# RWKV attention, Fourier mix and MLP on one core: ScalarE copies transposes as fp32 words, batch 3's transform in half columns, a new order

## Chip, core and metric

The kernel runs on one core of one Trainium2 chip. The metric is the device time of one execution in microseconds (us), the median of three runs. The engines are TensorE (PE; its weight loads are shown as PEld), VectorE (DVE), ScalarE (ACT), GpSimd (POOL) and SyncE (SP), which here only issues DMAs.

## The reference

Four batches, 8 heads, 768 positions, head size 48 (model size 384). A linear attention with decay gives x; then a Fourier mix over positions and model dimension, a layer norm and a two-layer MLP:

```python
cur = np.einsum('bhd,bhe->bhde', u[None] * kt, vt)
y[:, :, t] = np.einsum('bhd,bhde->bhe', rt, state + cur)
state = wt[:, :, :, None] * state + np.einsum('bhd,bhe->bhde', kt, vt)
...
X = np.fft.fft(x, axis=1)
X = np.fft.fft(X, axis=2)
u = x + np.real(X).astype(np.float32)
mu = np.mean(u, axis=-1, keepdims=True)
var = np.mean((u - mu) ** 2, axis=-1, keepdims=True)
un = (u - mu) / np.sqrt(var + 1e-06)
ch = np.maximum(un @ w_ch1, 0.0) @ w_ch2
return (u + ch).astype(np.float32)
```

## The kernel before

A program of some 1400 operations is written as data and then put out engine by engine. `op(engine, duration, function, r=..., w=...)` adds one; `r` and `w` name what it reads and writes, and from them the waits on semaphores follow. An operation may have alternatives on several engines. `ORDER` at the top lists for each engine (pe, act, dve, pool, sp) the numbers of its operations in the order in which they are put out; so it also says which engine does what. The durations in the text serve only to choose PSUM banks and the order of waits; the chip sees the order. Every engine works its list strictly in order.

**Start.** `small_constants`, `tables`, `sines`, `masks`, `fills`, `mirrors` and `tables_end` make the cosine and sine tables CS and SS, the identity IDW and its negative NIDW, masks and zero padding; ScalarE loads one activation table for the sines (L1079) and a second for Ln and Exp (L683). PE first runs 16 matmuls on a filled part of W1 (L1086) and later, between other work, `NW` warm matmuls (L1118) whose results nobody reads.

**Attention** (`attention`, 24 chunks of 128 positions, six to a batch): loads of w, k, r, v by SP (L597); Ln of w on ScalarE; two matmuls that sum it (L761, L765) and two Exp; rk = r k u with its sum dc (POOL or DVE); rh = r times the one Exp (L799), kh = k times the other. rh and kh are transposed: for the first 18 chunks by PE (L815, L821), with a bf16 copy from PSUM to `rkt` by `evict` (L574 on ScalarE, L575 on VectorE); for the last six by a DMA (L807). Then scores (L831), their mask (L836, ah), the state (L857, L865), the output y (L887) and x (L896, called addX here, or a copy). `fold` adds and subtracts halves of x into xf.

**Mix** (`mix`, one batch): three tables' transform over positions on PE (L953 to L956), evicted to hcs and mirrored to hcr; then for each of six blocks kb of 128 positions the model-dimension transform: three matmuls of 384 columns (L980, j = 0, 1, 2) on the tables DTM. VectorE adds x with a sum over the row (L985, uf), un is uf less its mean (ScalarE or VectorE), ScalarE also squares it. un is transposed, in batches 0 and 1 by PE (L1015) and `evict`, in 2 and 3 by one DMA for three blocks (L1021) to `unt`. Then the up matmuls (L1044) for three blocks at once, ht = relu (L1052 on ScalarE, L1050 on VectorE), the down matmuls (L1063, four at a time), osb (L1069) and the out DMA (L1073). Attention of the next batches is mixed in between by the order.

Of the kernel before, what the change touches and what calls it, by code (L numbers as in the profile page):

```python
# [7 lines left out]
ALU = mybir.AluOpType  # L8
# [24 lines left out]
NW = 32  # L33

YPE = (0, 1, 2, 3, 4)

# [5 lines left out]
        "7 68 1414 1415 1416 60 95 97 94 122 1417 124 1418 62 106 121 107 149 1419 64 110 151 113 1420 134 "  # L42
        "133 1421 1422 148 176 115 137 178 1423 1424 1425 1426 116 160 175 142 140 161 203 188 205 187 1427 "
        "143 164 1428 191 1429 263 167 1430 169 202 230 1431 170 215 1432 1433 229 196 197 214 194 1434 241 "
        "1435 1436 218 240 421 423 221 420 223 244 1437 224 479 1438 1439 255 1440 256 257 247 264 450 449 "
        "258 265 432 452 481 259 271 272 1441 273 274 275 276 277 266 278 260 279 267 280 461 281 282 268 "
        "301 433 285 293 294 295 302 1442 286 287 303 1443 311 491 327 312 299 328 313 319 320 462 291 321 "
        "1444 307 436 465 329 343 339 341 317 347 1445 337 325 345 333 359 478 355 353 382 392 386 507 394 "
        "351 398 439 378 508 510 519 380 349 357 490 442 376 384 520 542 494 390 388 396 366 541 468 367 471 "
        "544 368 523 371 553 574 497 575 372 554 361 362 529 526 557 405 500 585 406 586 363 764 373 560 562 "  # L50
        "589 765 767 407 410 794 796 793 411 400 592 776 401 615 599 402 805 783 777 412 600 601 616 780 617 "
        "602 618 603 619 604 620 621 622 607 608 822 609 610 611 623 624 625 626 612 823 637 825 629 655 630 "
        "638 852 639 645 854 631 646 656 647 812 806 835 657 834 643 671 663 672 673 635 664 651 665 838 809 "
        "886 888 689 683 687 691 703 685 864 681 669 695 885 786 851 693 699 841 701 815 697 897 863 705 661 "
        "898 919 706 867 901 707 715 844 677 870 918 873 1098 716 1099 1101 730 717 930 728 724 904 726 1125 "
        "722 929 906 734 710 1114 933 1177 711 1179 1127 1124 1151 1153 951 712 952 738 936 1111 720 740 959 "
        "742 960 953 1208 732 736 1210 943 961 1140 962 1150 963 944 1137 964 965 966 945 967 968 946 954 "
        "955 947 948 969 970 956 744 745 1166 1176 746 985 979 986 987 980 973 974 981 749 1006 975 1000 "
        "1238 1001 1007 1008 1002 994 995 996 750 754 1117 751 1189 1163 755 756 1023 1019 1237 1031 1025 "
        "1029 1021 1143 1015 1074 1068 1207 1195 1192 1033 1060 1056 1017 1169 1058 1062 1064 1037 1066 1249 "  # L60
        "1220 1072 1223 1027 1076 1035 1039 1259 1225 1040 1044 1045 1252 1049 1054 1050 1041 1260 1070 1261 "
        "1267 1262 1268 1263 1264 1275 1078 1276 1277 1269 1278 1279 1280 1281 1282 1283 1270 1284 1285 1286 "
        "1271 1272 1083 1289 1290 1316 1301 1291 1302 1295 1303 1296 1297 1079 1317 1318 1322 1323 1088 1051 "
        "1089 1310 1324 1311 1090 1084 1046 1080 1331 1347 1312 1335 1343 1337 1333 1085 1345 1339 1351 1341 "
        "1349 1370 1353 1386 1355 1365 1360 1366 1361 1372 1356 1376 1390 1384 1378 1374 1357 1380 1382 1367 "
        "1394 1362 1392 1388 1395 1399 1404 1400 1396 1401 1405 1406 1409 1410 1411"),
    "act": (
# [1084 lines left out]
```

## Time and profile before

| | before |
|---|---|
| median of three runs | 184.25 us (183.04, 184.25, 184.69) |
| profiled execution: time | 183.65 us |
| profiled execution: span from first to last instruction | 181.8 us |
| busy: PE, DVE, ACT, POOL | 175.5, 150.2, 130.1, 107.8 us |
| granted TensorE clock | 1.00 throughout |
| HBM read and written | 23.59 and 4.72 MB |

The difference between the profiled execution's time and its span lies before the first and after the last instruction. A form's row gives line, engine, operation, what it writes and reads, count, busy us and mean ns of one. Matmul ends are modelled in the profile, and a matmul's own duration contains time in which the next one already runs; how fast they follow each other is read from their starts.

### The profile page before, as it was taken

To read this page: it belongs to the slowest core of one execution; us is meant where nothing else is said; L and a number is where in the kernel's file an instruction comes from. 1 tells how busy PE (TensorE), PEld (TensorE's weight loads), DVE (VectorE), ACT (ScalarE), POOL (GpSimd) and SP (SyncE) were. 2 spreads that over 40 slices of the span, in tenths; PEclk is the share of its full clock that TensorE was granted. 3 is DMA by queue.
4 is the path that set the end of the run, shared out by engine and by line. 5 is a ranking of instruction groups with operands and counts; after the bars stand their busy time and mean duration, and the time that the engine had idled before them with its cause. 6 is when DMAs were issued, how large, how long until landed. Compare 5 with 4: busy or idle time off the path is not lost.

```text
span 181.8 us, 4574 instructions
## 1 busy us (share of the span) xinstructions
PE 175.5 (97%) x1718; PEld 115.8 (64%) x1718; DVE 150.2 (83%) x351; ACT 130.1 (72%) x323; POOL 107.8 (59%) x127
## 2 busy tenths in 40 slices
PE   4999999999999999999999999999999999999994
PEld 2466766766666776776767666665656766666663
DVE  8989999988988999999899998999799941860434
ACT  2879899499987876899999985977972455481410
POOL 3059888798324999587989987799763220000000
PEclk9999999999999999999999999999999999999999
DMA  6999999999997989898999999999640004360033
GB/s 126 218 217 214 184 215 194 180 211 187 170 206 140 221 174 260 185 221 192 224 224 189 221 164 222 170 232 188 88 85 0 5 0 108 107 176 1 0 130 130
DMA packets 116119, 28.99 MB, mean 159 GB/s; under 512 B 111361, under 2 KB 116098, under 8 KB 116098
## 3 DMA queue, kind: packets, MB, share of 16 engines
q1 hardware_dynamic: 114514, 26.36, 71.4%
q0 software_dynamic: 1584, 2.36, 7.7%
q8 instruction: 13, 0.21, 0.5%
q14 instruction: 8, 0.07, 0.1%
HBM read 23.59 MB, written 4.72 MB: 156 GB/s over the span
## 4 chain that ended last, share of the span: by engine, by line
PE 72%; DMA 7%; POOL 6%; DVE 5%; ACT 4%; SPq 3%; issue 3%; DVEq 0%; POOLq 0%; ACTq 0%
PE bank L1063 23%; PE bank L1044 19%; PE bank L980 5%; DMA rkt<-rkh 5%; PE bank L1086 3%; PE bank L831 3%; PE bank L956 2%; PE bank L1118 2%; POOL rk L551 2%; POOL rkh L551 2%; DMA in_r<-in_r_dram 2%; SPq L597 2%; PE bank L815 2%; PE bank L887 2%; PE bank L877 1%
## 5 line engine op out<-in xcount | busy, mean ns | idle before, releaser
L1063 PE MATMUL bank<-w,ht 128*128 128x384 bf16 (+2 forms) x300 | 54.0, 319 | 0.0
L1044 PE MATMUL bank<-unt,w 128*128 128x384 bf16 x288 | 53.6, 326 | 0.0
L1052 ACT ACTIVATE ht<-bank 128x384 bf16<-128x384 f32 x71 | 32.9, 500 | 16.3 <-PE bank L1044 15.9
L1063 PEld LDWEIGHTS bank<-w,ht 128*128 128x128 bf16 x300 | 27.7, 98 | 15.6 <-ACT ht L1052 0.2
L1044 PEld LDWEIGHTS bank<-unt,w 128*128 128x128 bf16 x288 | 26.7, 98 | 15.9 <-DVE osb L1069 0.4
L836 DVE TENSOR_TENSOR ah<-bank,msk 128x512 bf16<-128x512 f32 x48 | 31.1, 682 | 0.8 <-PE bank L831 0.5
L551 POOL TENSOR_TENSOR rkh<-in_k,e 128x384 bf16<-128x384 f32 x20 | 20.2, 1012 | 15.1 <-ACT e L780 12.4
L551 POOL TENSOR_TENSOR rk<-rk,ub 128x384 f32<-128x384 f32 x21 | 21.5, 1027 | 5.4 <-DVE rk L551 5.0
L1069 DVE SCALAR_TENSOR_TENSOR osb<-bank,rstd,uf 128x384 f32<-128x384 f32 (+2 forms) x25 | 14.8, 597 | 10.3 <-PE bank L1063 9.0
L551 POOL TENSOR_TENSOR vtd<-in_v,dc 128x384 f32<-128x384 f32 x21 | 17.6, 842 | 4.9 <-DMA in_v<-in_v_dram 3.0
L551 POOL TENSOR_TENSOR rk<-in_r,in_k 128x384 f32<-128x384 f32 x18 | 18.7, 1047 | 2.1 <-DMA in_r<-in_r_dram 2.1
L1050 DVE TENSOR_SCALAR ht<-bank 128x384 bf16<-128x384 f32 x25 | 13.3, 550 | 7.9 <-PE bank L1044 7.8
L985 DVE SCALAR_TENSOR_TENSOR uf<-bank,x 128x384 f32<-128x384 f32 x24 | 12.9, 553 | 2.9 <-PE bank L980 2.4
L565 ACT ACTIVATE xf<-uf,agg 128x384 bf16<-128x384 f32 x24 | 14.7, 616 | 0.6 <-DVE uf L985 0.6
L551 POOL TENSOR_TENSOR sd<-x 128x385 f32<-128x385 f32 x12 | 12.8, 1089 | 3.3 <-DVE x L896 3.2
L799 DVE TENSOR_TENSOR rkh<-bank,in_r 128x384 bf16<-128x384 f32 x24 | 13.2, 548 | 1.0 <-ACT bank L767 1.0
L780 ACT ACTIVATE e<-bank 128x392 f32<-128x392 f32 (+1 forms) x24 | 11.9, 498 | 2.7 <-PE bank L774 1.2
L767 ACT ACTIVATE bank<-bank 128x384 f32<-128x384 f32 x24 | 11.8, 496 | 2.6 <-PE bank L761 2.4
L788 DVE TENSOR_REDUCE dc<-rk 128x8 f32<-128x384 f32 x24 | 12.8, 543 | 1.1 <-POOL rk L551 1.1
L574 ACT ACTIVATE rkt<-bank 128x512 bf16<-128x512 bf16 x21 | 12.5, 602 | 1.6 <-PE bank L821 1.6
L565 ACT ACTIVATE lb<-in_w 128x384 bf16<-128x384 f32 x24 | 12.5, 529 | 1.3 <-DMA in_w<-in_w_dram 1.2
L565 ACT ACTIVATE un<-uf,agg 128x384 bf16<-128x384 f32 x18 | 10.2, 607 | 2.3 <-DVE uf L985 2.3
(138 smaller groups left out, 352.4 us busy)
## 6 DMA issues: line engine op xcount, KB each, us to landing
in_w<-in_w_dram SPq DMA_DIRECT2D x24, 192.0 KB, 3.8
in_k<-in_k_dram SPq DMA_DIRECT2D x24, 192.0 KB, 3.8
in_r<-in_r_dram SPq DMA_DIRECT2D x24, 192.0 KB, 3.8
in_v<-in_v_dram SPq DMA_DIRECT2D x24, 192.0 KB, 4.0
out_dram<-osb SPq DMA_DIRECT2D x23, 192.0 KB, 2.6
w<-in_moe_w_ch_dram POOLq DMA_DIRECT2D x2, 576.0 KB, 7.9
w<-in_moe_w_ch_dram POOLq DMA_DIRECT2D x1, 1152.0 KB, 12.0
out_dram<-osb SPq DMA_DIRECT2D x1, 128.0 KB, 1.7
```

The costliest lines, as they stand in the source:

```text
L551: return lambda e: e.tensor_tensor(out=o, in0=a, in1=b, op=f)
L565: return lambda e: e.activation(o, a, f, **kw)
L574: {"act": lambda e: e.activation(o(), i(), ACTF.Copy), "dve": lambda e: e.tensor_copy(out=o(), in_=i())}, **kw)
L788: op("dve", v_1(DM), lambda e: e.tensor_reduce(out=dc[:, :], in_=rku[:, :, :], axis=mybir.AxisListType.X, op=ALU.add), r=[("RK", i2)], w=[ ...
L799: op("dve", v_1(DM), lambda e: e.tensor_tensor(out=rh[:, :, 0:D], in0=ps(tce)[:, 0:DM].rearrange("t (h d) -> t h d", d=D), in1=rt[:, :, :] ...
L836: masked[n] = op("dve", v_1(512), lambda e, x=x: e.tensor_tensor(out=ah[:, x:H:2, :], in0=ps(ta[x])[:, :].rearrange("p (h t) -> p h t", t= ...
L985: op("dve", v_1(DM) + 60, lambda e, kb=kb, t=t: e.scalar_tensor_tensor(out=uf[:, kb, :], in0=ps(t)[:, 0:DM], scalar=1.0, in1=xb[:, kb, 0:D ...
L1044: ins = e.matmul(ps(t)[:, 0:384], W1[:, m, 256 * (j // 2) + j % 2:256 * (j // 2) + 256:2], unt[:, :, m, :], start=(m == 0), stop=(m == NM ...
L1050: {"dve": lambda e, j=j, t=t, ht=ht: e.tensor_scalar(out=ht[:, j, :], in0=ps(t)[:, 0:384], scalar1=su, scalar2=0.0, op0=ALU.mult, op1=ALU. ...
L1052: "act": lambda e, j=j, t=t, ht=ht: e.activation(ht[:, j, :], ps(t)[:, 0:384], ACTF.Relu, scale=su)},
L1063: ins = e.matmul(ps(t)[:, 0:hi - lo], ht[:, j, 128 * x:128 * x + 128], W2[:, j, lo:hi], start=(j == 0), stop=(j == NJ - 1))
L1069: op("dve", v_1(hi - lo) + 64, lambda e, kb=kb, t=t, o=o, lo=lo, hi=hi: e.scalar_tensor_tensor(out=o[:, lo:hi], in0=ps(t)[:, 0:hi - lo], s ...
```

## The change

1. `evict` on ScalarE: where the copy is bf16 to bf16 (x = 2), input and output are taken as fp32, so two bf16 values travel as one word and the instruction has half as many elements. The identity IDW is now also made by such a copy, on ScalarE, from NIDW, which VectorE fills with the identity first.
2. Table steps (TQ, zero fills, the mirrored tables, the negated ones and NIDW) get a ScalarE alternative. The two activation-table loads get a fence: each waits for the instruction before it on ScalarE.
3. For batch 3 the model-dimension transform works in half columns (193 instead of 384): j = 0 goes into one half of a PSUM bank, j = 2 into the other, j = 1 into both with two scaled copies DTC and DTS of its table. ScalarE copies the second half to SBUF, VectorE adds it for the first 193 columns and subtracts it, mirrored, for the others, and then adds x as before, from SBUF.
4. `NW` goes from 32 to 36, and the order of all engines is made anew. ScalarE now has 32 rkt and 11 unt copies (21 and 7 before), VectorE 4 and 1 (15 and 5).

```diff
-NW = 32
+NW = 36
+HALF_OUT = (3,)
...
+            for d, o in zip(self.order[e], self.order[e][1:]):
+                if o.fence:
+                    o.deps.add(d)
...
-        return op(None, {"act": a_ps(n) + more, "dve": v_1(n) if x == 1 else v_2(n)},
-                  {"act": lambda e: e.activation(o(), i(), ACTF.Copy),
+        def pair(a):
+            return a.bitcast(FP32) if x == 2 else a
+        return op(None, {"act": a_ps(n // x) + more, "dve": v_1(n) if x == 1 else v_2(n)},
+                  {"act": lambda e: e.activation(pair(o()), pair(i()), ACTF.Copy),
...
-        dset(384, ts(IDW[:, :], CI[:, :], 0.0, None, ALU.is_equal), r=["CI"], w=["IDB"])
+        dset(384, ts(NIDW[:, :], CI[:, :], 0.0, None, ALU.is_equal), r=["CI"], w=["NIDW"])
+        op("act", a_sb(192), lambda e: e.activation(IDW[:, :].bitcast(FP32), NIDW[:, :].bitcast(FP32), ACTF.Copy),
+           r=["NIDW"], w=["IDB"])
...
+    def flip(o, i, sg, **kw):
+        f = ts(o, i, sg, None, ALU.mult)
+        return op(None, {"pool": 740, "dve": 260, "act": a_sb(3 * HQ)},
+                  {"pool": f, "dve": f, "act": act(o, i, ACTF.Copy, scale=sg)}, port=("dve",), **kw)
...
+               {"dve": f, "pool": f, "act": act(TQ[:, q, :], KI[:, :], ACTF.Identity, scale=TN[:, q:q + 1], bias=MGC[:, :])},
...
+        DTC, DTS = CN[:, 0, :], SN[:, 0, :]
+        if b in HALF_OUT[:1]:
+            for z, T in enumerate((DTC, DTS)):
+                op(None, {"act": a_sb(HE), "dve": v_2(HE)},
+                   {"act": lambda e, z=z, T=T: e.activation(T, DTM[:, 1, 0:HE], ACTF.Copy, scale=CQ[:, z:z + 1]),
...
+            if b in HALF_OUT:
+                t = g.tile("f")
+                for j in (0, 2, 1):
+                    def f(e, j=j, kb=kb, t=t):
+                        a = 128 * (kb % NP)
+                        x = (hcs if kb < NP else HCR)[:, j, a:a + 128]
+                        if j != 1:
+                            return e.matmul(ps(t)[:, (HE if j else 0):(2 * HE if j else HE)], x, DTM[:, j, 0:HE], start=(j == 0),
+                                            stop=False, skip_group_check=True)
+                        e.matmul(ps(t)[:, 0:HE], x, DTC, start=False, stop=True, skip_group_check=True)
+                        return e.matmul(ps(t)[:, HE:2 * HE], x, DTS, start=False, stop=True, skip_group_check=True)
...
+                if b in HALF_OUT:
+                    fs = SD[:, kb % 2, 0, 0:HE]
+                    op("act", a_ps(HE), lambda e, t=t, fs=fs: e.activation(fs, ps(t)[:, HE:2 * HE], ACTF.Copy),
+                       r=[t], w=[("SD", kb % 2, 0)])
+                    op("dve", v_1(HE), lambda e, kb=kb, t=t, fs=fs: e.tensor_tensor(
+                        out=uf[:, kb, 0:HE], in0=ps(t)[:, 0:HE], in1=fs, op=ALU.add),
+                       r=[t, ("SD", kb % 2, 0)], w=[("UFa", i, kb), ("UF", i, kb)])
+                    op("dve", v_1(HE), lambda e, kb=kb, t=t, fs=fs: e.tensor_tensor(
+                        out=uf[:, kb, DM - 1:HE - 1:-1], in0=ps(t)[:, 1:HE - 1], in1=fs[:, 1:HE - 1], op=ALU.subtract),
+                       r=[t, ("SD", kb % 2, 0)], w=[("UFb", i, kb), ("UF", i, kb)])
...
```

## The prediction

> **What bounds the kernel.** I read the busy shares first, then the windows, the chain of waits, the forms of each line, and the timeline of the last batch.
>
> ```profile
> PE 175.5 (97%) x1718; PEld 115.8 (64%) x1718; DVE 150.2 (83%) x351; ACT 130.1 (72%) x323; POOL 107.8 (59%) x127
> PE   4999999999999999999999999999999999999994
> DVE  8989999988988999999899998999799941860434
> ACT  2879899499987876899999985977972455481410
> ```
>
> TensorE (PE) is busy from the second slice to the last. To see whether that is real I took start-to-start times of its matmuls in the timeline: from 40 us on they follow each other at their own pace, with under 3 us of holes in 142 us. So from there on only columns that PE no longer streams, or holes, move the end. Before that it is different:
>
> ```profile
> 8.20:32.50 24.30, 24.02 (x302) 16.24 (x302) 22.63 (x47) 20.56 (x47) 19.57 (x25) 1.00 1.04 206
> 60.00:130.00 70.00, 69.26 (x767) 47.37 (x766) 65.88 (x142) 59.40 (x152) 60.43 (x63) 1.00 1.01 201
> 143.00:182.00 39.00, 36.21 (x246) 23.09 (x244) 18.13 (x42) 15.14 (x41) 1.76 (x2) 1.00 0.26 76
> L1118 PE MATMUL bank<-idw,msk 128*128 128x384 bf16 x32 | 9.0, 327 | 0.0
> ```
>
> (Columns: length, then busy us of PE, PEld, DVE, ACT, POOL, clock, DMA share, GB/s.) In the first window PE also looks full, but it holds most of the 32 warm matmuls, which compute nothing. There VectorE (DVE) is busy 22.63 of 24.30 us: it paces batch 0's attention, ScalarE (ACT) is next. In the last window both idle more than half of the time.
>
> **The sum.** It is made against the profiled execution: span 181.8 us, time 183.65 us, so 1.85 us lie around the span. That execution is 0.6 us under the median of the runs shown (184.25) and inside their spread (183.04 to 184.69); I add nothing for this.
>
> **ScalarE copies as fp32 words.** The rows:
>
> ```profile
> L574 ACT ACTIVATE rkt<-bank 128x512 bf16<-128x512 bf16 x21 | 12.5, 602 | 1.6 <-PE bank L821 1.6
> L767 ACT ACTIVATE bank<-bank 128x384 f32<-128x384 f32 x24 | 11.8, 496 | 2.6 <-PE bank L761 2.4
> L574 ACT ACTIVATE unt<-bank 128x384 bf16<-128x384 bf16 x7 | 3.2, 494 | 0.0
> L575 DVE COPY rkt<-bank 128x512 bf16<-128x512 bf16 x15 | 6.1, 415 | 0.2 <-PE bank L821 0.2
> ```
>
> 384 elements cost ScalarE 494 ns as bf16 and 496 as fp32, 512 cost 602: it pays by element, 0.83 ns each. 256 words should take 602 - 256 x 0.83 = 390 ns, 192 words 335. The bounds are 214 ns (its two-column row, L929) and 602. The new order gives ScalarE 32 rkt and 11 unt copies instead of 21 and 7; 32 x 0.39 + 11 x 0.335 = 16.2 us against 12.5 + 3.2 = 15.7, so ScalarE itself saves nothing in total. VectorE loses 11 rkt copies (415 ns) and 4 unt (352 ns), 6.0 us, and takes pieces from GpSimd (POOL), which does 10 fewer. Counting each order with its rows, between batch 0 and batch 3's fold VectorE goes from 118.3 to 118.9 us, ScalarE from 111.9 to 112.1, POOL loses 8 us of 88. PE hides all of this after 40 us: **0**. Without that cover, POOL's part of the chain at 79 to 101 us would be worth up to the 0.7 us of PE idle between 90 and 120 us.
>
> **Start-up.** Up to the addX (L896) of batch 0's last chunk VectorE has 88 instructions in either order. Neighbours overlap by 0.08 us (a 0.55 us instruction is followed after 0.47), so each is taken with its duration less 0.08: three rkt copies less, -1.0; two table steps TQ now on ACT, -0.46; two fills less, -0.15; one rh product moved behind, -0.47; one fold more, +0.5; one vb copy, +0.27; a table negation, +0.35; five small new instructions, +0.5. Sum -0.46. ScalarE, from its first Ln on: eight copies of 0.52 become eleven of 0.31, -0.75; one negation and one vb copy fewer, -1.1; one fill, +0.15; -1.7. Since VectorE is the fuller, I take **-0.5**; the bounds are -1.2, where the load of v for chunk 5 stops it, and +0.5. That load stands two places later in SP's queue (k one place): at 0.95 us a place (192 KB at about 206 GB/s) it lands near 29 us instead of 27, and the consumer in ACT's queue ran at 28.66 and VectorE's vtd at 30.70, so up to about 1.2 us of gain fits.
>
> The new first steps of ScalarE stand ahead of the sine table's load. Two TQ, fills and the identity copy end near 3.5 us (VectorE's ten instructions before the identity add up to 2.3 us from 0.81, the copy 0.21 to 0.52), the load (its new fence waits for that copy; behind it stand the sines, the second load and the first Ln) takes 1.28, so sines can start at about 5.1; before, they waited until then anyway:
>
> ```profile
> ACT ss L565 <- DVE uf L559: 3.2, 1, 3.2
> 5.21 0.69 ACT L565 ACTIVATE ss<-uf 128x582 bf16<-128x582 f32 x1 [3.21 <-DVE uf L559]
> 6.80 1.28 ACT L683 ACT_TABLE_LOAD   x1
> 8.17 0.94 ACT L565 ACTIVATE lb<-in_w 128x384 bf16<-128x384 f32 x2
> ```
>
> The 3.2 us wait hides it: 0, and at most +0.5 if every new copy takes 0.52.
>
> A page speaks against this. The Trainium skill, "ScalarE: Activation LUTs", What ACT_TABLE_LOAD costs, gives a switch 1283 ns and about 1380 ns of drain; by it the sines would start some 1.1 us later and the start-up gain would turn into a loss. The trace's second load is followed by the next ScalarE instruction 0.09 us after its 1.28 us, so no drain stands there, and I keep 0.
>
> **Warm matmuls.** 36 instead of 32. W1's fill is now second on VectorE, so the 16 early ones start near 1.3 us instead of 2.48, and three warm ones precede the bonus. Those cover idle time. Behind the point where PE has work enough (some 35 us) stand two, before five; each takes 0.163 us, so -0.5 to 0: **-0.2**.
>
> **Batch 3 in half columns.** Per block three matmuls of 384 columns become four of 193. Rows:
>
> ```profile
> 147.33 1.30 PE L980 MATMUL bank<-dtm,hcs 128*128 128x384 bf16 x7
> 145.43 0.92 PE L956 MATMUL bank<-ss,xf 128*128 128x193 bf16 x9
> ```
>
> Seven take 1.30 us with the last one's 0.326: (1.30 - 0.326) / 6 = 0.162 each. Nine of 193 columns with weight loads of their own: (0.92 - 0.246) / 8 = 0.084. So 6 x (3 x 0.162 - 4 x 0.084) = **-0.9**; a far bound is +1.0, if a half cost as much as a whole.
>
> The Trainium skill, "TensorE: Matmul & The Clock Gate", LDWEIGHTS, gives a weight load of 128 columns 128/1.2 = 107 ns. By that four pieces would take 0.43 us and the saving would be 0.36. The 0.084 above, beside weight loads of 97 ns in the same rows, is the measurement, and it decides.
>
> For this each block adds a ScalarE copy of 193 columns (496 - 191 x 0.83 = 337 ns) and two VectorE instructions of 193 columns. No row is the same; between L799 (384 columns, 548 ns) and L836 (512, 682) a column costs 1.05 ns, so 348 ns, and the 191-column fold at 31.16 us took 0.35. Bounds 350 and 548. They stand in the queue ahead of un and of the transposing DMA, whose landing releases batch 3's first up (L1044):
>
> ```profile
> 150.96 1.29 SPq L1021 DMA_TRANSPOSE unt<-un  x1
> 154.81 1.14 PE L1044 MATMUL bank<-unt,w 128*128 128x384 bf16 x6
> ```
>
> From the first finished block: copy and hand-over 0.55; on VectorE nine halves (0.27), one ht (0.47), three full sums (0.56), one un (0.33): 4.9; DMA issue 0.1 and landing 3.3 (median of this DMA): 8.9 us. PE meanwhile has, by its new order, 2.2 us up to the last piece of the third block and then ten down pieces (L1063, 0.65) and four transforms, 7.1: 9.3 us. Cover holds by 0.4 us: **0**. Behind that DMA in SP's queue stand batch 2's last out DMAs; they wait as long, and only osb buffers wait for them. At the upper bounds (halves at 0.47, landing 4.2) it lacks 2.3 us.
>
> Sum: -0.5 - 0.2 - 0.9 = -1.6; 183.65 - 1.6 = 182.05, rounded to 182.1.
>
> **Rivals.** **More at the start** (182.1 - 0.7 = 181.4, down to 180.6): ACT's 1.7 us less work carries through to the limit of 1.2. For it: the chain holds ACT pieces at 28.3 to 30 us; against: VectorE's 93%.
>
> **Start-up stays** (183.65 - 0.9 + up to 0.8 = 183.2 around): the new waits eat the 0.5, and warm matmuls delay work.
>
> **Batch 3's cover fails** (the other side): the halves cost near full width, VectorE's twelve more instructions hold un, the DMA and also the down banks, whose osb stand behind them. From 2.0 us of stall the kernel is slower than its own 183.65; 2.3 us, and up to 1.2 more if a bank held by a late osb (twelve halves at 0.2 us extra put it 2.4 us back) stops PE too, gives 183.65 - 0.9 + 2.3 = 185.05 to 186.3 without a start-up gain. Against: VectorE sat idle 2.37 us just before its first uf there.
>
> **The words are not cheaper** (cost by bytes): eleven start-up copies at 602 are 2.3 us more on ACT, and 43 in all 9 us; 183.65 + 2.3 - 0.9 = 185 to 187. The 494 and 496 ns rows speak against it.
>
> **From cases to numbers.** Forecast 0.42, more at the start 0.18, start-up stays 0.16, cover fails 0.18, words not cheaper 0.06. About 1% can be told from no change here: below 182.4 is faster, above 186.1 slower. Faster: 0.30 of the forecast's 0.42, 0.17 of the second case and 0.01 = 0.48. Slower: 0.10 of the failing cover and 0.05 of the words = 0.15. Same: the remaining 0.37. The range, 180.6 to 185.8, leaves out the ends of the first and last two rivals; the forecast's own is 181.3 to 183.2.
>
> **What would show it.** rkt copies on ACT at 0.39 us; sines at 5.1 to 5.3; x of batch 0's last chunk written near 31.4 instead of 31.89; transform pieces of batch 3 at 0.084; no hole ahead of batch 3's first up; tail after the last matmul as before. A later x, a hole of over 0.4 us before that up, or ScalarE copies near 0.6 would make it wrong.

## The result, and the profile after

| | before | after |
|---|---|---|
| median of 20 runs each | 183.59 us (181.55 to 185.29) | 185.14 us (183.5 to 186.52) |
| ratio | | 1.0096, interval 1.0069 to 1.0123 |
| profiled execution: time, span | 183.65, 181.8 us | 183.69, 181.8 us |

The change makes the kernel about 1% slower; 182.1 us, faster, was forecast. The profiled execution of after is one of its two quickest. Its span is that of before: what the change saves is lost again inside. A second profiled execution, at 186.13 us, lies on the other side of the median and somewhat nearer to it; I call it "after, again" and use it for what the first one does not show.

The page of after, the lines that answer those shown of before; then the three windows (length, busy us of PE, PEld, DVE, ACT, POOL, clock, DMA share, GB/s), and the warm matmuls' row:

```profile
PE 175.8 (97%) x1728; PEld 116.2 (64%) x1728; DVE 158.1 (87%) x364; ACT 131.2 (72%) x348; POOL 100.4 (55%) x114
PE   7989999989999999999999999999999999999994
DVE  5989999889999999999999999999999899644433
...
L1180 PE MATMUL bank<-idw,msk 128*128 128x384 bf16 x36 | 10.2, 340 | 0.0
```

```profile
8.20:32.50 24.30, 23.50 (x286) 15.19 (x286) 23.32 (x52) 19.02 (x49) 17.95 (x21) 1.00 1.04 202
60.00:130.00 70.00, 69.35 (x753) 47.33 (x752) 68.36 (x143) 59.29 (x162) 56.72 (x58) 1.00 0.95 192
143.00:182.00 39.00, 36.18 (x255) 23.58 (x252) 22.39 (x56) 14.74 (x42) 2.38 (x2) 0.99 0.26 76
```

VectorE is busy 158.1 us instead of 150.2, for 13 instructions more; 4.3 us of this stand in the last window, where batch 3's halves are. GpSimd lost 7.4 us. In the first window ScalarE gave up 1.5 us, VectorE gained 0.7, and it is VectorE that paces this stage. In the middle window VectorE has 2.5 us more, for one instruction more.

To see what PE does I split its span by the starts of its matmuls: useful ones at the pace of their shape (the 20th percentile of its start-to-start times in these five executions), warm ones with all the time up to the next start, and what is left, the loss. The level of a column depends on the pace taken, the differences between rows hardly do. "Freed" and "freed, 30 warm" are versions from the experiments (f3 and g1).

| us | useful | warm | loss | loss 36–44 | 44–60 | 75–100 | 100–125 |
|---|---|---|---|---|---|---|---|
| before | 153.5 | 10.8 | 12.5 | 0.65 | 0.92 | 2.21 | 2.86 |
| after | 152.6 | 12.5 | 12.7 | 1.57 | 0.93 | 2.60 | 2.32 |
| after, again | 152.6 | 12.5 | 14.9 | 1.56 | 1.84 | 3.74 | 1.73 |
| freed (f3) | 152.6 | 12.5 | 12.2 | 0.87 | 0.95 | 2.77 | 2.29 |
| freed, 30 warm (g1) | 152.6 | 11.6 | 13.1 | | | | |

The 0.9 us that the half columns were to save are in the first column, to the tenth. The last two windows are read together: what is late in one can be caught up in the next. In g1 idle time that warm matmuls filled before counts as loss.

The same split tells how far PE's useful work is behind that of before at a given time. At 35 us it is 0.96 us behind in after and 0.87 in after, again; at 44 us 1.17 in both; at 140 us 1.01 and 3.14. So the start costs about 1 us in both executions, and after, again loses another 2 us between 44 and 140 us.

**The start.** VectorE's last step of batch 0's attention, x of its sixth chunk, first in the timeline of before, then of after (start, length, engine, line; the bracket is idle time before it and what ended it):

```profile
31.89 0.55 DVE L896 TENSOR_TENSOR x<-bank,vtd 128x384 f32<-128x384 f32 x1
```

```profile
13.24 1.05 POOL L560 TENSOR_TENSOR rkh<-in_k,e 128x384 bf16<-128x384 f32 x1 [0.97 <-ACT e L808]
13.36 1.35 DVE L560 TENSOR_TENSOR rk<-rk,ub 128x384 f32<-128x384 f32 x1
...
22.06 0.92 DVE L560 TENSOR_TENSOR xf<-x 128x191 bf16<-128x191 f32 x1
...
25.62 0.98 DVE L560 TENSOR_TENSOR rkh<-in_k,e 128x384 bf16<-128x384 f32 x1
...
32.99 0.56 DVE L924 TENSOR_TENSOR x<-bank,vtd 128x384 f32<-128x384 f32 x1 [0.38 <-PE bank L915]
```

It comes 1.1 us later, where 0.5 earlier was forecast. The rk at 13.36 is a product of 128x384 that took 560 ns in before; here GpSimd's product began 0.12 us ahead of it, and VectorE's ended 0.42 us after GpSimd's. Three such pieces (13.36, 22.06, 25.62) took 1.8 us more than their short forms; before has none ahead of its x. The 88 VectorE instructions up to this x, each at the shortest duration of its shape in the two traces, less 0.08 us, make 26.0 us in before and 25.2 in after: the forecast saving is there, and larger. What they take above their shortest durations rises from 2.3 to 3.4 us, and VectorE's idle time from 2.7 to 3.5; at 3.50 us it waits 1.27 us for a table step that ScalarE now makes. After is ahead at first: the products rh of the first two chunks start at 9.63 and 11.42 us, in before at 10.97 and 12.90. The three held pieces stand behind that point.

**The middle.** After, around 38 us, and then after, again:

```profile
37.36 0.52 POOL L1005 COPY hcr<-hcs 128x384 bf16<-128x384 bf16 x1
...
37.53 1.73 DVE L560 TENSOR_TENSOR rk<-in_r,in_k 128x384 f32<-128x384 f32 x1
37.84 1.00 POOL L560 TENSOR_TENSOR rkh<-in_k,e 128x384 bf16<-128x384 f32 x1
...
39.80 0.34 PE L1029 MATMUL bank<-dtm,hcr 128*128 128x384 bf16 x1 [0.57 <-DVE uf L1044]
```

```profile
60.17 1.14 PE L1125 MATMUL bank<-w,ht 128*128 128x384 bf16 x6 [0.86 <-ACT lb L574]
...
89.63 0.99 POOL L560 TENSOR_TENSOR rk<-in_r,in_k 128x384 f32<-128x384 f32 x1
...
89.76 2.65 DVE L565 TENSOR_SCALAR un<-uf,agg 128x384 bf16<-128x384 f32 x1
...
90.58 1.60 POOL L560 TENSOR_TENSOR vtd<-in_v,dc 128x384 f32<-128x384 f32 x2
...
92.47 0.34 PE L1077 MATMUL bank<-idw,un 128*128 128x128 bf16 x3 [1.33 <-DVE un L565]
```

The same pattern: VectorE's instruction, both inputs in SBUF or a table step from SBUF, starts just behind one of GpSimd's and lasts past the end of two or three of them. Six residual adds (uf) stand behind the rk, and PE waits for a bank that they free. The un of 2.65 us has a mean of 460 ns in before; PE stands 1.33 us for it. The 0.86 us at 60.17 is put down to ScalarE's lb, which was long done: it is the second half of the weights W2. GpSimd issues that transfer, at 44.13 us in before and at 47.93 in after, again, because it first waits 6.91 us for a VectorE piece, and it lands 12.1 us later.

Before has such holds too. The longest are 1.32 us for a fold at 111.63 and this one, just behind the stage that the prediction counted:

```profile
33.24 1.60 DVE L551 TENSOR_TENSOR xf<-x 128x191 bf16<-128x191 f32 x1
```

The same fold took 0.35 us at 31.16. Beside this one GpSimd runs two pieces, from 33.05 to 34.61 us. So the trace from which VectorE's steps were priced had the price of a hold in it.

The mean durations carry the same story (x is the count), but for the last row, in which before has its 1.60 us:

| VectorE | before | after |
|---|---|---|
| rk = r k | 563 ns x6 | 675 x10 |
| rk times u | 560 x3 | 777 x4 |
| vtd | 554 x3 | 828 x4 |
| un | 460 x6 | 569 x7 |
| kh | 546 x4 | 633 x5 |
| fold of 191 columns | 766 x3 | 466 x5 |

### The profile page after: what moved, and what is told of

Read it like the earlier page. It is cut to its first block, busy times and chain, and to the rows that moved or that the text cites. A ratio compares the mean times of both kernels' runs of the same rounds, so it can differ in the third digit from the quotient of the medians.

```text
span 181.8 us, 4612 instructions
## 1 busy us (share of the span) xinstructions
PE 175.8 (97%) x1728; PEld 116.2 (64%) x1728; DVE 158.1 (87%) x364; ACT 131.2 (72%) x348; POOL 100.4 (55%) x114
## 4 chain that ended last, share of the span: by engine, by line
PE 80%; DVE 11%; ACT 6%; issue 1%; DVEq 0%
PE bank L1125 24%; PE bank L1106 23%; PE bank L991 4%; PE bank L1148 3%; PE bank L859 3%; PE bank L1029 3%; PE bank L915 2%; PE bank L912 2%; DVE rk L560 2%; PE bank L1180 2%; DVE ah L864 2%; PE bank L789 2%; PE bank L843 2%; PE bank L905 2%; PE bank L793 2%; PE bank L885 1%
## 5 line engine op out<-in xcount | busy, mean ns | idle before, releaser
L1125 PE MATMUL bank<-w,ht 128*128 128x384 bf16 (+2 forms) x300 | 52.6, 320 | 0.0
L1114 ACT ACTIVATE ht<-bank 128x384 bf16<-128x384 f32 x67 | 30.3, 494 | 7.7 <-PE bank L1106 7.7
L560 POOL TENSOR_TENSOR rk<-rk,ub 128x384 f32<-128x384 f32 x20 | 19.8, 1000 | 16.3 <-DVE rk L560 9.0
L560 POOL TENSOR_TENSOR rkh<-in_k,e 128x384 bf16<-128x384 f32 x19 | 19.1, 1008 | 10.4 <-ACT e L808 8.9
L1112 DVE TENSOR_SCALAR ht<-bank 128x384 bf16<-128x384 f32 x29 | 15.3, 549 | 5.9 <-PE bank L1106 5.9
L588 ACT ACTIVATE rkt<-bank 128x256 f32<-128x256 f32 x32 | 11.7, 384 | 6.3 <-PE bank L849 5.7
L560 POOL TENSOR_TENSOR rk<-in_r,in_k 128x384 f32<-128x384 f32 x14 | 14.2, 1022 | 0.3 <-DMA in_r<-in_r_dram 0.3
L816 DVE TENSOR_REDUCE dc<-rk 128x8 f32<-128x384 f32 x24 | 12.7, 543 | 0.3 <-POOL rk L560 0.2
L560 POOL TENSOR_TENSOR sd<-x 128x385 f32<-128x385 f32 x9 | 10.1, 1138 | 4.2 <-DVE x L924 4.1
L574 ACT ACTIVATE vb<-in_v 128x384 bf16<-128x384 f32 x22 | 11.5, 523 | 1.1 <-DMA in_v<-in_v_dram 1.1
L574 ACT ACTIVATE lb<-in_w 128x384 bf16<-128x384 f32 x24 | 12.1, 525 | 0.1
```

Source lines behind the costliest of these rows:

```text
L560: return lambda e: e.tensor_tensor(out=o, in0=a, in1=b, op=f)
L574: return lambda e: e.activation(o, a, f, **kw)
L588: {"act": lambda e: e.activation(pair(o()), pair(i()), ACTF.Copy), "dve": lambda e: e.tensor_copy(out=o(), in_=i())}, **kw)
L816: op("dve", v_1(DM), lambda e: e.tensor_reduce(out=dc[:, :], in_=rku[:, :, :], axis=mybir.AxisListType.X, op=ALU.add), r=[("RK", i2)], w=[ ...
L1112: {"dve": lambda e, j=j, t=t, ht=ht: e.tensor_scalar(out=ht[:, j, :], in0=ps(t)[:, 0:384], scalar1=su, scalar2=0.0, op0=ALU.mult, op1=ALU. ...
L1114: "act": lambda e, j=j, t=t, ht=ht: e.activation(ht[:, j, :], ps(t)[:, 0:384], ACTF.Relu, scale=su)},
```

## The experiments

Unless it says otherwise, the figure behind the name is the median with the ratio to before and its interval. A diff of the order shows the operation that moves; all other places stay.

### Which part of the change

**after, again** is one more profiled execution of the changed kernel itself: 186.13 us.

> The changed kernel, unaltered, for a second trace: the profiled execution took 183.69 us (span 181.8), the median is 185.14. Theory S (start-up): the trace shows the same places with x of batch 0's last chunk near 33.6 us, and the missing 1.5 us lies ahead of 35 us, where every engine is near its limit. Rival M (middle): start-up as in the first trace, and more holes on PE between 60 and 130 us. Rival H (half columns): a hole ahead of batch 3's first up matmul.

What it showed stands above: 0.9 us at the weights, 1.3 at the un, together about the 2.1 us by which its span exceeds that of after.

**Full columns** (n1), the new order with batch 3's transform as before: 185.87 us, 1.0146 (1.0099 to 1.0194).

```diff
-HALF_OUT = (3,)
+HALF_OUT = ()
```

> The changed kernel with batch 3's transform in full columns as before (20 operations taken out of the order, nothing else moved). Theory S: the half columns save PE 0.9 us and their cover holds, so this takes 0.9 us longer than the changed kernel, about 186.0, ratio to before 1.014. Rival H (the half columns cost more than they save in most executions): 184.5 or less, ratio 1.005 or under.

The medians put half columns at 0.7 us; the intervals overlap, so that figure alone settles nothing, but PE's useful time goes from 152.6 to 153.5, the 0.9 us of the sum.

**bf16 copies** (p1), the new order with ScalarE copying bf16: 187.24 us, 1.0227 (1.0188 to 1.0266). **Words in the old order** (w1), before with nothing but the words: 183.21 us, 0.999 (0.9962 to 1.0018).

```diff
-            return a.bitcast(FP32) if x == 2 else a
+            return a
```

```diff
+        def pair(a):
+            return a.bitcast(FP32) if x == 2 else a
...
-                  {"act": lambda e: e.activation(o(), i(), ACTF.Copy),
+                  {"act": lambda e: e.activation(pair(o()), pair(i()), ACTF.Copy),
```

> The changed kernel with ScalarE's copies of transposes as bf16 elements again (0.60 instead of 0.38 us for 512), order unchanged. If the words help where ScalarE is busy: 11 such copies in the start-up are 2.4 us more on ScalarE, of which it was idle some, so 0.5 to 1.5 us longer than the changed kernel, 185.6 to 186.6. If PE's order hides them throughout: 185.1, the same as the changed kernel.

> The kernel before, order unchanged, with ScalarE's copies of transposes as fp32 words. ScalarE gets 21 x 0.21 + 7 x 0.16 = 5.5 us shorter. If the words are worth something by themselves it is in the start-up, 8 copies, up to 1.5 us: 182.1 to 183.2. If VectorE paces the start-up, as the prediction had it: 183.4 to 183.6, ratio 0.998 to 1.

In the old order words are worth nothing that can be measured; in the new one 2.1 us (187.24 - 185.14). The new order gives ScalarE 43 copies and needs them short; the words pay for the reordering and not beyond it. p1 came out above both of its expectations.

**Words and half columns in the old order** (h1): 186.94 us, 1.0186 (1.0145 to 1.0226). The edit is the words above and the half-column diff, each new operation behind the one that it serves.

> The kernel before, in its own order and assignment to engines, with the two features of the change alone: ScalarE's bf16 copies as fp32 words, and batch 3's model-dimension transform in half columns (the six half copies on ScalarE, the twelve half adds on VectorE put where the six full adds stood). 32 late warm matmuls as before. Theory O (the two features are sound, the new order costs the time): 183.6 - 0.9 = 182.7 us, the half columns at 0.9 and the words at 0. Rival F (the features are what costs): no faster than before, 183.6 to 185.

PE's timeline in it:

```profile
150.50 2.12 PE L1106 MATMUL bank<-w,ht 128*128 128x384 bf16 x12 [1.28 <-DVE uf L1022]
156.78 1.14 PE L1087 MATMUL bank<-unt,w 128*128 128x384 bf16 x6 [1.22 <-DMA unt<-un]
```

Here is the prediction's rival "cover fails", in the old order: with three smaller ones, of 0.62, 0.25 and 0.24 us, these holes make 3.6 us. So half columns need an order that keeps down matmuls back for the chain to the transposing DMA. In after they are there: no hole stands ahead of batch 3's first up, at 155.59.

h1 came out above both of its expectations, and it shows one thing more. Its x of batch 0's sixth chunk starts at 31.18 us, 0.7 earlier than in before, and PE's useful work is 0.88 us ahead of before's at 35 us; at 60 us it is 0.16 behind. A lead from the start is not carried through to the end in that order, as the sum let it be.

### Repairs that missed

**Weights earlier** (e1): 187.17 us, 1.0176 (1.0134 to 1.0218). **One un to ScalarE** (e2): 185.26 us, 1.0101 (1.0055 to 1.0146). **Both** (e3): 186.2 us, 1.0134 (1.0091 to 1.0176).

```diff
 pool: ... rkU, rk, W2 second half, ...      (e1, e3)
-  W2 issued behind the product that waits for VectorE
+  W2 issued ahead of it
 un of the block held at 89.76               (e2, e3)
-  dve: un
+  act: un
```

> The changed kernel with one entry of GpSimd's list moved: the transfer of the second expert matrix (1.15 MB) is issued before the two recurrence products that wait for VectorE, so at about 39 us instead of 47.9 us. Theory W (the weight arrives too late): in the typical execution of the changed kernel the first down-projection matmul waits from 59.3 to 60.2 us, and the transfer issued at 47.9 us landed 12.1 us later, at 60.0; in before it was issued at 44.1. Issued at 39 it lands by 52, the matmul starts at 59.3, and the time falls by 0.9, from 185.1 to about 184.3. Rival, the queues are full anyway between 33 and 57 us (180 to 220 GB/s): then 1.15 MB ahead of batch 1's inputs makes these up to 5 us later, and the time stays at 185.1 or rises to 186.

> The changed kernel with one instruction moved from VectorE to ScalarE: the normalised row block 5 of batch 1 (un<-uf,agg, 128x384, from SBUF to SBUF), which took 2.65 us on VectorE in the typical execution, 1.06 in the quick one and 0.41 elsewhere, while GpSimd ran three instructions back to back beside it. Theory P (VectorE is held off SBUF while GpSimd runs): on ScalarE it takes 0.61 us whatever GpSimd does, TensorE's hole of 1.33 us at 91 us is gone, and the time falls by 1.0 to 1.4, to about 183.9. Rival, VectorE is behind there for its total load: TensorE waits for the next of its instructions instead and the time falls by no more than 0.4.

> Both edits in one, the early transfer and the block on ScalarE. If the late weight and the held VectorE are two separate losses that the new order brought to the typical execution, they add: 0.9 + 1.3 = 2.2 us, so 182.9 us, and the kernel is then faster than before (183.6). If they are one loss seen twice (what one hole gives back, the next one takes), the sum stays at the larger one, 183.9.

e1's windows and PE's timeline:

```profile
44.00:60.00 16.00, 13.99 (x126) 8.55 (x123) 13.17 (x28) 12.51 (x35) 8.27 (x9) 1.00 1.11 206
```

```profile
53.57 0.66 PE L1106 MATMUL bank<-unt,w 128*128 128x384 bf16 x3 [1.80 <-ACT ht L1114]
```

The weights came in time (issued at 39.48 us, landed 12.2 us later), and the loads of the next chunks came later: in this window GpSimd waits 4.0 us and ScalarE 2.3 for loads of v, and neither does in after, again. The DMAs already moved 195 GB/s there, here 206, so 1.15 MB put in earlier delayed the rest. The stall moved from 60 to 53 us; PE stood 2.01 us in this window, against 0.70 in after, again. e1 and e3 are slower than either theory had it. In e2 the held un was gone, and the next of its kind took the place, in VectorE's timeline:

```profile
90.47 1.72 DVE L565 TENSOR_SCALAR un<-uf,agg 128x384 bf16<-128x384 f32 x1
```

with a PE hole of 1.19 us behind it. Taking away one stall did not help; the next runs take away more of what makes them.

### Pieces taken off VectorE where GpSimd runs

**rk to GpSimd** (f1), the product held at 37.53: 184.23 us, 1.0066 (1.0037 to 1.0096). **Two un to ScalarE** (f2), both of those held around 90: 184.18 us, 1.0043 (1.0017 to 1.0069). **All three** (f3): 183.94 us, 1.0032 (1.0003 to 1.0061).

```diff
-dve: rk of batch 1's first chunk            (f1, f3)
+pool: the same, behind the piece before it
-dve: un of two blocks of batch 1            (f2, f3)
+act: the same, beside the un of their neighbours
```

> The changed kernel with one product of batch 1 (rk<-in_r,in_k of chunk 0) given back from VectorE to GpSimd, behind the memset after which GpSimd idles for 6.9 us. On VectorE it began at 37.46 us, GpSimd began an instruction 0.3 us later, and it took 1.73 us instead of 0.55; batch 0's six residual adds stand behind it. Theory P (VectorE is held while GpSimd runs): the first residual add starts at 37.6 to 38.0 instead of 39.1, TensorE's hole of 0.56 us at 39.2 is gone, the first up-projection matmul comes at 42.7 instead of 43.6; the end moves by 0 to 0.9, by 0 if the weight that lands at 60.0 us takes it back. Rival (VectorE is simply full there): the residual adds start no earlier than 38.7 and the up-projection at 43.3 or later.

> The changed kernel with both normalised blocks of batch 1 that VectorE made (blocks 5 and 3, un<-uf,agg) moved to ScalarE, since with one moved the other took its place: it was the 1.72 us instruction at 90.5 us, again until GpSimd paused. Theory P: no VectorE instruction between 86 and 95 us is longer than 0.7 us, TensorE's hole at 91 us is gone, and the time falls by 1.0 to 1.5 from 185.1, to 183.6 to 184.1. Rival (it is the load on VectorE and ScalarE together): ScalarE, busy 9.5 of 10 us there, passes the 1.0 us on to TensorE, and the time stays within 0.4 of 185.1.

> All three instructions moved, the product to GpSimd and the two blocks to ScalarE. If the holds are the loss of the new order, the sum: 185.1 - 0.9 - 1.3 = 182.9 us, or 183.8 if the second expert matrix, landing at 60.0, takes back the first. If they aren't, 184.7 to 185.5.

In f1 PE's loss between 36 and 44 us falls from 1.56 to 0.88 and the first up starts at 42.98 instead of 43.6. In f2 the loss between 75 and 100 us is 2.76, against 3.74 in after, again; but after's quick execution has 2.60 without the edit, so this figure alone says little. The spans' medians tell it more plainly than the times: 183.3 us in after, 182.4 in f1, 182.2 in f2 and 181.5 in f3. That is the span of before, but f3's time does not follow: 2.46 us lie around the span (median of 12) where before has 1.80. That was new, and the next runs are about it.

### The time around the span

In before, 1.74 to 1.86 us lie between span and time, always. In after 4 of 20 executions have over 1.9, up to 2.73; in f3 9 of 12, up to 2.99. The DMA view of f3 from 180 us on, and the same view of g1, below:

```profile
core 0 of [0], span 181.3 us
DMA  8710000000000000000000004000000000000000
...
q8 instruction: 1, 0.02, 1.1%
```

```profile
core 0 of [0], span 181.2 us
DMA  9500000000000000000000000000000000000000
```

The slices are 0.125 us: in f3 one transfer of instructions stands at 183.1 us, 1.8 us behind the last instruction, and in g1 nothing does. Such a transfer, of 16 KB, is there in the profiled executions of after, after again, e2, e3, f1 and f3, which have 1.89 to 2.53 us around the span, and not in those of before, n1, e1, f2, h1 or g1, which have 1.79 to 1.81. p1 does not fit: it has 2.06 and no transfer. If it is the next piece of TensorE's program, six matmuls fewer should take it away.

**Freed, 30 warm** (g1), f3 without its last six warm matmuls: 182.93 us, 0.9986 (0.9961 to 1.0012). **After, 30 warm** (g2): 184.53 us, 1.007 (1.0042 to 1.0098).

```diff
-NW = 36
+NW = 30
```

> The kernel with three instructions freed, without the last six of its 36 warm matmuls (two of them stand in a dense stretch of TensorE at 41 and 42.3 us, four between 28.7 and 32.2 us beside idle time). Two effects: 0.33 us of TensorE's dense stretch, and TensorE's program is shorter by 6 matmuls with their weight loads. Theory I (the last fetch of 16 KB of instructions, which ends 2 us behind the span, is what makes the time outside the span 2.0 to 3.0 us in 8 of 12 executions instead of 1.8): with the program shorter the fetch isn't started, the time outside the span is 1.75 to 1.86 in every execution, and the median falls by 0.66 + 0.33, from 183.94 to 182.9. Rival (the outside time varies for another reason): some executions stay above 2.0, and the median falls by 0.3 at most. A second rival: the clock drops without the matmuls at 28.7 to 32.2 us, and the time rises.

> The changed kernel without the same six warm matmuls and with nothing else changed. Theory I: time outside the span 1.75 to 1.86 in all executions (the changed kernel has 4 of 20 above 1.9). Late warm matmuls: the two at 41 and 42.3 us cost 0.33 where TensorE is dense, unless the second expert matrix, landing at 60, takes it back. So 185.14 to 184.7 to 185.1.

In all 24 executions 1.75 to 1.85 us lie around the span, and in the 12 of the next version too. g1 is the best version found, 2.2 us under after and equal to before. n1, whose program on TensorE is six matmuls shorter than after's because of its full columns, has 1.75 to 1.84 in all six executions. That the fetch is TensorE's I conclude from these edits, and for g1 and g2 they touch no other engine's list; which instructions it brings the trace does not tell. Nor is it shown how the fetch makes the execution longer: in f3 it ends 2.77 us behind the last instruction, and only 2.53 lie around the span.

**Start freed too** (g3): g1 with two of the pieces that VectorE took over at the start given back to GpSimd: 183.13 us, 0.9997 (0.9969 to 1.0024).

```diff
-dve: kh and rk times u of batch 0's second chunk
+pool: the same
```

> As the kernel with three instructions freed and six warm matmuls fewer, and besides two pieces of batch 0's chunk 1 (rkh<-in_k,e and rk<-rk,ub, 0.54 and 1.35 us on VectorE between 12.9 and 14.7 us) given back to GpSimd, ahead of chunk 2's rkh<-in_k,e. Theory P: VectorE gains 1.9 us less 0.3 of its own waits, and since it is busy 24 of 25 us between 8 and 33.5 us the last x of batch 0 is written 0.8 to 1.5 us earlier, at 32.0 to 32.7 instead of 33.5, and the kernel ends 0.5 to 1.0 earlier than its sibling with the same six matmuls fewer: about 182.2. Rival (chunk 2's rkh is then 1 us later and sets the pace): x of batch 0 stays at 33.3 to 33.8 and the time is that of the sibling.

In VectorE's timeline of g3 the rk at 13.36 is gone, and others are held:

```profile
12.46 1.28 DVE L559 TENSOR_TENSOR rk<-in_r,in_k 128x384 f32<-128x384 f32 x1
...
15.32 0.88 DVE L559 TENSOR_TENSOR rk<-in_r,in_k 128x384 f32<-128x384 f32 x1
```

They took 0.49 and 0.54 us in g1. x of the sixth chunk starts at 32.89 us, in g1 at 32.78. A busier GpSimd holds the pieces that stay; the start-up loss is not got back by moving two of them.

### VectorE and GpSimd by themselves

Four kernels leave the whole computation out but the instructions in question. **m1** runs eight forms of VectorE instruction three times alone and three times beside six GpSimd products.

```diff
+    forms = [ts(o16[0], a[0], AGG[0][:, 0, 0:1], None, ALU.subtract), tt(o32[0], a[0], a[1], ALU.mult),
+             ..., tt(o32[0], BANK[0][:, 0:384], a[0], ALU.add), ...]
+    pf = tt(po[0], p[0], p[1], ALU.mult)
...
+            if beside:
+                for x in range(6):
+                    q = op("pool", 950, pf, w=["po"])
```

> A kernel that computes nothing of the reference (it writes zeros): eight forms of VectorE instruction on 128x384, three of each alone and then three beside six products on GpSimd (128x384 fp32, 0.95 to 1.0 us each, back to back). Theory P: forms that read and write SBUF alone are held while GpSimd runs, those with two fp32 inputs or a fast mode (fp32 to bf16 by a scalar, bf16 copies) above all: the three take 3 to 6 us from first to last instead of 1.4; forms that read PSUM take their 0.55 us as before. GpSimd's own durations stay at 1.0. Rival (each gets its turn): at most one GpSimd instruction of delay for one of VectorE, so 1.5 us each for all forms from SBUF, and GpSimd's instructions become longer too.

VectorE's timeline, three un alone and beside, and three sums of a PSUM bank and an SBUF tile alone and beside:

```profile
9.99 1.33 DVE L492 TENSOR_SCALAR un<-x,agg 128x384 bf16<-128x384 f32 x3 [0.20 <-POOL vtd L499]
11.52 3.39 DVE L492 TENSOR_SCALAR un<-x,agg 128x384 bf16<-128x384 f32 x3 [0.20 <-POOL vtd L499]
...
53.61 1.74 DVE L488 TENSOR_TENSOR uf<-bank,x 128x384 f32<-128x384 f32 x3 [4.32 <-POOL vtd L499]
55.55 1.74 DVE L488 TENSOR_TENSOR uf<-bank,x 128x384 f32<-128x384 f32 x3 [0.20 <-POOL vtd L499]
```

| one VectorE instruction, 128x384, ns | alone | beside GpSimd's products |
|---|---|---|
| table step, SBUF fp32 to bf16 (un) | 420 | 1033 to 1253 |
| product of two SBUF tiles, fp32 to fp32 or to bf16 | 557 | 1232 (the first, 558) |
| sum of two SBUF tiles, bf16 | 358 | 1031 to 1036 (the first, 358) |
| cast, SBUF fp32 to bf16 | 360 | 1031 to 1035 (the first, 361) |
| reduce from SBUF | 553 | 553 |
| sum of PSUM and SBUF | 558 | 557 |
| table step from PSUM | 558 | 557 |

So it goes by form, and in this kernel VectorE gets its turn after every GpSimd instruction; GpSimd's own products, where VectorE went first, go from 992 ns to 1163 to 1365. The Trainium skill, "SBUF — State Buffer", Who interferes with whom, states the forms: VectorE and GpSimd share one pair of SBUF ports, whoever issues first has it for its whole instruction, a VectorE instruction with two SBUF inputs meets a GpSimd instruction that reads SBUF there, one in a two-port mode meets GpSimd too, one with at most one SBUF input outside those modes does not, and a reduce never does. The table agrees on the forms if un and the cast, with one SBUF input each, ran in such a mode; their 420 and 360 ns alone, against 553 to 558 for the other fp32 rows, fit that, but no trace names the mode. Who goes first is not settled by the starts: the first product, bf16 sum and cast began 0.04 to 0.05 us ahead of GpSimd's product and were not held, and the first un began 0.04 ahead and was.

One turn explains the 1.35 us at 13.36, not the 2.65 at 89.76. Three more kernels looked for that. **m2** writes GpSimd's products to three tiles in turn, so that they start 0.95 us apart and leave no gap; **m3** puts GpSimd's own mix there, a product and two products with a broadcast factor, and starts un at twelve offsets; **m4** adds 84 loads of inputs.

```diff
-                    q = op("pool", 950, pf, w=["po"])
+                    q = op("pool", 950, tt(po[x % 3], p[0], p[1], ALU.mult), w=[("po", x % 3)])
```

```diff
+        for x, f in enumerate([big, bc[0], bc[1]] * 2):
+            q = op("pool", 950, f, w=[("po", x % 3)])
+        for x, f in enumerate([fill(OSB[2][:, 0:32 * n + 8], 0.0), red, un, acc, un2]):
```

```diff
+    for x in range(84):
+        op("sp", 620, lambda e, n=n, i=i, bb=bb, cc=cc: e.dma_start(INB[n][i][:, :, :],
+            src[n][bb, :, cc * CH:(cc + 1) * CH, :].rearrange("h t d -> t h d")), w=[("in", n, i)], ...)
```

> The measurement of the eight VectorE forms again (it writes zeros and computes nothing of the reference), with one difference: GpSimd's six products write three tiles in turn, so that they follow one another without the wait for the one before (in the first measurement they began 1.07 us apart and took 0.99). Theory S (VectorE gets in only where GpSimd pauses): beside them the first of the three held instructions takes until GpSimd's run ends, 3 to 5.5 us, and the next two 0.4 to 0.6. Rival (each gets its turn): 1.0 to 1.25 us each as in the first measurement. Forms that read PSUM, and the reduction, stay at 0.55.

> A third measurement by itself (zeros are written, nothing of the reference is computed): twelve times, GpSimd runs a product, two products with a broadcast factor, and the three again, back to back, and VectorE a memset of 8 to 360 columns (to shift the phase), a reduction, the block un<-x,agg, an instruction that reads PSUM, and the block again. Theory B (beside the products with a broadcast factor VectorE gets no turn between two GpSimd instructions): some of the 24 blocks take 1.7 to 2.7 us, those that begin beside the first product or the first broadcast one. Rival (one turn for each GpSimd instruction, always): all 24 take 0.42 to 1.3 us, and what held the block in the kernel stays open.

> The measurement with GpSimd's mixed sequence once more (fourteen times; zeros are written, nothing of the reference is computed), with 84 input loads of 192 KB running beside it, as the kernel has them (some 200 GB/s). Theory D (writes of transfers into SBUF take VectorE's turn between two GpSimd instructions): some of the 28 blocks take 1.3 to 2.7 us, where without transfers the longest took 0.78. Rival (transfers don't matter to these engines): all 28 stay at 0.42 to 0.85 us, and the hold of 2.65 us remains unexplained.

m3's timeline, and a window of m4 (it has no PE, so its columns are DVE, POOL, clock, DMA share, GB/s):

```profile
39.54 0.66 DVE L493 TENSOR_SCALAR un<-x,agg 128x384 bf16<-128x384 f32 x1
39.95 1.84 POOL L488 TENSOR_TENSOR vtd<-uf,dc 128x384 f32<-128x384 f32 x2
```

```profile
30.00:60.00 30.00, 10.47 (x25) 29.00 (x38) 1.00 1.08 212
```

m2 still gives one turn each (1.03 to 1.25 us), un takes 0.46 to 0.78 us in m3 and 0.50 to 0.79 in m4. None of them makes an un of 1.7 us or more. Gapless GpSimd work, broadcast operands and full DMA queues are therefore not enough, each in the form tried. Why VectorE passes up two or three turns in the kernel stays open.

## Why the prediction was wrong

Against the quick profiled execution (182.05 forecast, 183.69 measured) one term of the sum fails, the start-up. Against the median (185.14) a second one adds about as much, the 0 for the middle.

- **Start-up, -0.5: measured +1.1 at x, and PE's useful work about 1 us behind at 35 us.** This is the step that failed. The count of VectorE's work had the right sign (-0.46 forecast, -0.8 at shortest durations). What failed is the price: each instruction was taken by rows of before in which it was hardly held. Three of before's pieces with two SBUF inputs overlap GpSimd by over 0.2 us there (18.56, 23.85 and 24.41 us), and they took 0.55 to 0.64. The change takes pieces from GpSimd, whose inputs lie in SBUF, and gives them to VectorE while GpSimd goes on with its others; three that met one took 0.4 to 0.8 us more each. Some of VectorE's freed time also became idle time. The bounds of the term, -1.2 to +0.5, looked at loads and at instruction counts and had no hold in them. No run takes the holds of the start away without making others (g3), so their share in the 1.1 us is read from the trace and not shown by an edit. The prediction named the rival "start-up stays", at 183.2, for new waits and warm matmuls; its time is near the quick execution's and a new wait is there, but the holds are not in it.
- **"PE hides all of this after 40 us: 0."** The second step that failed: the cover does not hold against a step that is held for 1.7 to 2.7 us, and the median span is 1.5 us above the quick one's (183.3 against 181.8). The forecast had VectorE's load in the middle about unchanged; with the holds it has 2.5 us more in the middle window. In the quick execution PE loses 0.9 us more at 36 to 44 us and gets part of it back later; in after, again 0.9 at the weights and 1.3 at one un come on top. f1, f2 and f3 show the cause by taking it away: three of 364 VectorE instructions elsewhere, 1.2 us less (185.14 to 183.94). f3's interval lies clear of after's, f2's touches it and f1's overlaps it.
- **Words at 390 and 335 ns: right.** Measured, in the groups of after:

```profile
L588 ACT ACTIVATE rkt<-bank 128x256 f32<-128x256 f32 x32 | 11.7, 384 | 6.3 <-PE bank L849 5.7 <-PE bank L843 0.4
...
L588 ACT ACTIVATE unt<-bank 128x192 f32<-128x192 f32 x11 | 3.2, 335 | 0.1
```

  That they change nothing was right in the old order (w1). In the new one they are worth 2.1 us, which the sum could not see, as it took order and words together.
- **Sines at 5.1: right, at 5.18**, though by another way than told. ScalarE's timeline of after begins with a table load that the diff does not show, 0.72 us into the span; the copies behind it are quick enough:

```profile
0.72 1.28 ACT L574 ACT_TABLE_LOAD   x1 [0.72 <-PEq L1199]
...
3.67 1.28 ACT L1141 ACT_TABLE_LOAD   x1
4.97 0.31 ACT L574 ACTIVATE rkh<-tc 128x128 bf16<-128x128 f32 x1
5.18 0.68 ACT L574 ACTIVATE ss<-uf 128x582 bf16<-128x582 f32 x1
```

  The copy behind the second load starts 0.02 us after the load's end; the drain that the Trainium skill, "ScalarE: Activation LUTs", What ACT_TABLE_LOAD costs, states does not show here either.
- **Half columns, -0.9 and cover held: right.** 153.5 to 152.6 us of useful PE time, and the halves cost what was summed (337 ns on ScalarE, 348 on VectorE):

```profile
L1041 DVE TENSOR_TENSOR uf<-bank,sd 128x191 f32<-128x191 f32 x6 | 2.1, 354 | 0.1
L1038 DVE TENSOR_TENSOR uf<-bank,sd 128x193 f32<-128x193 f32 x6 | 2.0, 356 | 0.3 <-ACT sd L1036 0.3
L1036 ACT ACTIVATE sd<-bank 128x193 f32<-128x193 f32 x6 | 2.0, 331 | 2.9 <-PE bank L1021 2.5 <-DVE uf L1041 0.3
```

  h1 shows that the rival was real where the order does not keep work back.
- **Warm matmuls, -0.2: inside its range by count.** Behind 35 us before has four (37.6 to 43.7 us) and after two (41.07 and 42.34), 0.33 us less. What the term did not have is the length of TensorE's program, ten matmuls more (four warm, six of the half columns), which goes with the instruction fetch at the end: without six of them g1 is 1.0 us under f3 at the median, and g2 0.6 under after.
- **"1.85 us lie around the span", kept as a constant.** It is one in before. In after and its relatives it goes up to 3.0.

The chance of slower was 0.15, all of it on batch 3 and the words; the way in which it came was not among the rivals.

## What to carry to other kernels

Price an instruction that is moved to VectorE by whether its operands are all in SBUF and whether GpSimd is at work in that stage: rows from a quiet stage are then only a lower bound, and a GpSimd instruction's length is the price to put beside it. Moving work off GpSimd relieves nothing if its remaining work holds the engine that takes over: here three such pieces, given to ScalarE or back to GpSimd, were worth 1.2 us. Look for such a hold in the trace at hand before pricing: before had one of 1.60 us. And look at the time around the span as well as at the span: a longer program can pay behind its last instruction.

## What was not expected of the hardware

- A VectorE step whose operands lie in SBUF took 1.72, 1.73 and 2.65 us beside two or three GpSimd instructions (and a fold in before 1.60), where such a step takes 0.35 to 0.56 alone; by itself the pair of engines takes turns one by one (1.03 to 1.25 us). The difference is open.
- In six profiled executions a 16 KB instruction transfer begins 1.1 to 1.9 us after the last instruction, and up to 1.2 us more lie around the span in such kernels. With six TensorE matmuls fewer the time around the span was 1.75 to 1.85 us in 36 of 36 executions, and the three profiled ones have no such transfer.
- A transfer of weights issued 8.5 us earlier made the kernel slower (e1 against after: 1.0176 against 1.0096 of before, some 1.5 us), where the DMAs were already moving 195 GB/s.
